# One filler unit moved from the end of one attention batch to the start of the next

## Chip, cores and metric

The kernel runs on one core of one Trainium2 chip. The metric is device time in microseconds (us). Before the change it was 326.37 us, the median of three runs (326.36 to 327.01).

A ratio in this document is the mean time of one kernel's fast runs over that of the other's fast runs of the same rounds, with a 95% interval. It is therefore not quite the ratio of the medians that are quoted beside it.

## The reference

Eight batches of sparse attention (8 heads, 576 tokens, head size 64, a window of 32 to each side, and 8 global tokens that see and are seen by all) are followed by a two-layer product with a squared relu over all 4608 tokens.

```python
scores = scale * np.matmul(q, k.transpose(0, 1, 3, 2))
mask = np.abs(pos[:, None] - pos[None, :]) <= window
mask = mask | is_global[:, None] | is_global[None, :]
...
attn_out = np.matmul(softmax(where(mask, scores, -1e9)), v)     # abridged
x = attn_out.transpose(0, 2, 1, 3).reshape(B * S, H * D)        # 4608 x 512
h = x @ w_in                                                     # 512 -> 2048
r = np.maximum(h, 0.0)
out = (r * r) @ w_out                                            # 2048 -> 512
```

## The kernel before

Attention works on pairs of heads, four pairs to a batch. It makes TensorE wait often: scores go to PSUM, ScalarE takes their exponential, VectorE masks them, and only then can TensorE multiply them with the values. The two-layer product is almost pure TensorE work. So its pieces, called **units**, stand in a queue and are taken as filler between the steps of a pair. A unit is four 128x512 matmuls: `mm1` makes 128 of the 2048 inner columns for a chunk of 512 tokens, `mm2` a quarter of one 128-row block of the result.

```python
def unit(i, n, nxt=None, then=None):                 # pair i; n = units taken at three places
    scs = [scores(i, half, pair_tag[half], WIN2) for half in range(2)]   # PSUM tiles sc, acc
    et = [weights(half, scs[half], WIN2) for half in range(2)]           # Exp, then mask
    ...
    take(n[0])
    ...
    for half in range(2):
        acc = outputs(i, half, et[half], pair_tag[half], WIN2, ...)      # sc, acc again
        finish_outputs(i, half, acc, ...)                                # to xT in SBUF
        if half == 0:
            take(n[1])
    if i % NHP == NHP - 1:
        scatter(i // NHP)                            # global tokens' columns into xT
    take(n[2])
```

A chunk has 512 tokens and a batch 576. Chunk 0 needs batch 0 alone, but chunk 1 needs the tokens of batch 1 as well: its first `mm1` can't run before batch 1's last outputs are in xT and the scatter is done. Whatever is left of a batch's queue is flushed at the batch's end.

```python
queue += units[1] + units[2]              # with one kept: 25 units of chunk 0
...
for hp in range(NHP):                     # batch 1
    unit(NHP + hp, SCHED["b1"][hp], ...)
...
for b in range(2, B):
    queue += units[b + 1]                 # 32 units of the next chunk
    for hp in range(NHP):
        n = ((2, 1, 4), (3, 1, 4), (2, 1, 5), (2, 1, 6)) if b < B - 1 else SCHED["last"]
        unit(NHP * b + hp, n[hp])
        ...
    take(99)
```

The end of an output half, as far as the argument needs it (VectorE executes in this order):

```python
# finish_outputs, second half of a batch's last pair (cut)
act.activation(out=rec[r], in_=av[xs][rs, :, 0:GTOK], func=AF.Ln)         # L702
act.activation(out=rec, in_=rec, func=AF.Exp, scale=-1.0)                 # L703
dve.tensor_reduce(out=gsum[b][...], in_=av[x][...], ...)                  # L720
dve.tensor_tensor(out=gs, in0=gsum[b][:, 0], in1=gsum[b][:, 1], ...)      # L726
global_outputs(b, gs, 0, NHP, columns)                                    # L690, L692
dve.tensor_tensor(out=xT[...], in0=av[x][...], in1=rec[r], op=ALU.mult)   # L732, last read of acc
# then scatter: eight small copies, L751; then the next pair's masks, L643
```

The softmax here doesn't subtract the row's maximum and nothing guards it: scores larger than these inputs give would overflow.

Of the kernel before, what the change touches and what calls it, by code (L numbers as in the profile page):

```python
# [39 lines left out]
)  # L40
W2 = 440
MB = (0, 456)
SCHED = dict(w8=2, w9=3, w5=3, w6=0, w7=4, wa=4, wb=3, wc=3, g0=1, w0=2, w1=4, w2=2, w3=2, w4=3, w=5, h0=0, h1=1, h4=1, h5=1, h2=1, h3=0, keep=1, b1=((3, 1, 3), (2, 1, 3), (2, 1, 3), (2, 1, 2)), last=((2, 1, 4), (3, 1, 4), (2, 1, 4), (2, 1, 7)))
ONES = 2.0**-7 * (1.0 + 15360.0 / 2**23)


# [1 line left out]
def kernel(  # L48
# [144 lines left out]
    def keep_warm(n):  # L193
        if n:
            w = pst("tr", [P, 512])
        for _ in range(n):
            nc.tensor.matmul(w, idle[:, 0:P], idle, start=True, stop=True)  # L197
# [8 lines left out]
    def indices():  # L206

        low = g64.bitcast(I32).rearrange("p (g two) -> p g two", two=2)[:, :, 0]
        clamped(g32c, 0, S - 1, low)
        nc.vector.tensor_copy(out=g16, in_=low)  # L210
        edges()
        gb = pst("mm", [P, 512])[:, 0:NG]
        nc.tensor.matmul(gb, ones, g16, start=True, stop=True)
        return gb
# [11 lines left out]
    def one_hots(gb):  # L226
        nc.vector.tensor_copy(out=gbf, in_=gb)
        nc.vector.tensor_tensor(
            out=oh, in0=gbf.unsqueeze(1).to_broadcast((P, NT, NG)),
            in1=tok.unsqueeze(2).to_broadcast((P, NT, NG)), op=ALU.is_equal,  # L230
        )
        nc.vector.tensor_tensor(
            out=ohp, in0=gbf.unsqueeze(1).to_broadcast((P, TJ, NG)),
            in1=tokp.unsqueeze(2).to_broadcast((P, TJ, NG)), op=ALU.is_equal,
        )
# [4 lines left out]
    def mask_natural(half):  # L240
        if 1:
            for t, so, c0, w in WIN[half]:
                for grp in range(4):
                    lo, hi = max(grp * GRP, c0), min(grp * GRP + GTOK, c0 + w)
                    o = MB[half] + so + lo - c0
                    if lo < hi:
                        u = lo - 8 * grp - KT * t + U0
                        nc.vector.tensor_copy(
                            out=mask[:, o : o + hi - lo], in_=ub[t // 4][:, u : u + hi - lo]
                        )  # L250
                    lo, hi = max(grp * GRP + GTOK, c0), min((grp + 1) * GRP, c0 + w)
                    o = MB[half] + so + lo - c0
                    if lo < hi:
                        nc.vector.tensor_copy(
                            out=mask[:, o : o + hi - lo],
                            in_=rows[:, t // 4 : t // 4 + 1].to_broadcast((P, hi - lo)),
                        )

    def mask_globals_matmul(half):
        mg = pst("acc" if half == 0 else "mm", [P, 1, 512])  # L260
        if 1:
            wins = [x for x in WIN[half] if x[3] > 8]
            for i, (t, so, c0, w) in enumerate(wins):
                o = c0 - half * BANKC
                nc.tensor.matmul(
                    mg[0:NG, 0, o : o + w], oh[:, t, :],
                    mask[:, MB[half] + so : MB[half] + so + w],
                    start=(i == 0), stop=(i == len(wins) - 1), skip_group_check=True,
                )
        return mg  # L270
# [161 lines left out]
    def cast_tokens(op, nm, hp):  # L432
        t = nat0[(nm, hp)] = sbt("nat0" + nm, [TP, TJ, P], FP16, bufs=2)
        op(out=t.rearrange("p j (h d) -> p h j d", h=2), in_=st[nm][0:TP, pair(hp)])
# [5 lines left out]
    def clear_value_rows():  # L440
        act.copy(
            out=vb[0][0:NG, :, 0 : 2 * H : 2],
            in_=idle[0:NG].rearrange("p (h d) -> p h d", d=D).unsqueeze(1).to_broadcast((NG, NT, H, D)),
        )
# [42 lines left out]
    def tr_k(i, op=None, tail=None, last=None, tag="mm", then=None):  # L487
        op = op or dve.tensor_copy
        tk, gl = transposed("k", i, tag)
        kt = kts[i % NHP]  # L490
        op(
            out=kt[:, 0:4, 8:P].rearrange("p t (q j) -> p t q j", j=TJ),
            in_=tk[:, 0:80].rearrange("p (t q) j -> p t q j", t=4),
        )
        if then:
            then()
        (tail or op)(
            out=kt[:, 4, 8 : 8 + KN[4]].rearrange("p (q j) -> p q j", j=TJ), in_=tk[:, 80:96]
        )
        (last or op)(out=kt[:, :, 0:NG], in_=gl.unsqueeze(1).to_broadcast((P, NT, NG)))  # L500

    def tr_q(i, op=None, tag="mm"):
        op = op or dve.tensor_copy
        tq, gl = transposed("q", i, tag)
        q4 = qts[i % NHP].rearrange("p (g x) -> p g x", x=GRP)
        op(
            out=q4[:, :, 0:GTOK].rearrange("p g (q j) -> p g q j", j=TJ),
            in_=tq.rearrange("p (g q) j -> p g q j", g=4),
        )
        op(out=q4[:, :, GTOK:GRP], in_=gl.unsqueeze(1).to_broadcast((P, 4, NG)))  # L510
# [252 lines left out]
    clear_value_rows()  # L763
    keep_warm(SCHED["w0"])
    gb = indices()
    fetch_globals()
    one_hots(gb)
    keep_warm(SCHED["w1"])
    mask_natural(0)
    mg = mask_globals_matmul(0)  # L770
    keep_warm(SCHED["w2"])
    cast_tokens(dve.tensor_copy, "k", 0)
# [5 lines left out]
    mg = mask_globals_matmul(1)  # L778
    keep_warm(SCHED["w3"])
    ets = {}  # L780

    def half0(i):
        tag = pair_tag[i % 2]
        ets[i] = exps(0, scores(i, 0, tag, WIN), WIN)
# [7 lines left out]
    cast_tokens(dve.tensor_copy, "q", 1)  # L792
    keep_warm(SCHED["w4"])
    tr_k(1, then=lambda: tr_q(1, act.copy))
    keep_warm(SCHED["w5"])
    tr_k(2, then=lambda: (half0(1), tr_q(2, act.copy)))
# [175 lines left out]
```

## Time and profile before

| | before |
|---|---|
| time, median | 326.37 us |
| TensorE busy | 316.8 us, 97% of the span |
| VectorE, ScalarE busy | 227.0 us (70%), 214.4 us (66%) |
| chain that ended last | 88% TensorE |
| a unit of four 128x512 matmuls | 0.86 us |
| stops of TensorE from the first second-product matmul (49.44 us) to the end | 0.20 us at 67.65 and 0.68 us at 69.50 |

A **stop** is here the distance of two matmuls' starts less what the first one takes when nothing is waited for (0.216 us for 512 columns); a change of matmul shape, which costs 0.10 us or less, is not counted. Stops are read from starts because a matmul's end in the profile is modelled. The list of waits counts from that end and so shows less, or nothing. The lines that matter are in the prediction.

### The profile page before, as it was taken

Reading aid. Unit: us, or ns where it says so; the run is one execution under the profiler, and the core shown is the slowest. Engines: PE = TensorE matmul, PEld = TensorE weight load, DVE = VectorE, ACT = ScalarE, POOL = GpSimd, SP = SyncE. Lnnn points to the kernel's source line nnn. Section 1 sums busy time; section 2 is a strip of 40 time slices with the busy share of each in tenths; the row PEclk is TensorE's granted clock in tenths of the full one; section 3 lists DMA queues with packets and bytes.
Section 4 is the critical chain, followed back from the end, with each engine's and each line's share of the span. In section 5 each row is a group of like instructions: output and inputs, shape, how many; then the busy total and the mean of one; then the engine's idle time right before and its main releaser. Section 6 shows DMA issues by size and latency. Waiting matters only on the chain.

```text
span 326.0 us, 6920 instructions
## 1 busy us (share of the span) xinstructions
PE 316.8 (97%) x2434; PEld 164.5 (50%) x2434; DVE 227.0 (70%) x674; ACT 214.4 (66%) x418; POOL 110.2 (34%) x148
## 2 busy tenths in 40 slices
PE   6998999999999999999999999999999999999996
PEld 2645775445555455455545544454455544444444
DVE  7786987677878875987598758885888675313421
ACT  6677985569954995499549954995499636404600
POOL 9824663639800870089107700680000000000000
PEclk9999999999999999999999999999999999999999
DMA  8999999999994999399959996999610011011012
GB/s 186 176 204 190 174 186 167 154 147 107 153 131 141 73 138 171 134 83 139 132 162 82 148 126 144 98 134 132 139 60 0 34 58 39 2 73 56 2 54 75
DMA packets 148229, 37.53 MB, mean 115 GB/s; under 512 B 136171, under 2 KB 143715, under 8 KB 148195
## 3 DMA queue, kind: packets, MB, share of 16 engines
q0 software_dynamic: 105168, 17.93, 78.9%
q1 hardware_dynamic: 42880, 19.04, 30.3%
q8 instruction: 19, 0.31, 0.4%
q10 hardware_dynamic: 146, 0.13, 0.1%
q14 instruction: 16, 0.12, 0.1%
HBM read 37.30 MB, written 17.05 MB: 167 GB/s over the span
## 4 chain that ended last, share of the span: by engine, by line
PE 88%; DVE 7%; ACT 2%; issue 1%; DMA 1%
PE mm L587 29%; PE mm L524 26%; PE tr L524 9%; PE tr L587 7%; PE sc L679 3%; PE acc L679 3%; PE sc L627 3%; PE mm L543 2%; PE acc L627 2%; DVE xT L751 2%; PE tr L197 1%; DVE vb L457 1%; PE sc L670 1%; DVE xT L732 1%; ACT rec L702 1%
## 5 line engine op out<-in xcount | busy, mean ns | idle before, releaser
L587 PE MATMUL mm<-w_out,gt 128*128 128x512 f16 x448 | 104.4, 379 | 0.0
L524 PE MATMUL mm<-xT,w_in 128*128 128x512 f16 x384 | 90.8, 379 | 0.5 <-DVE xT L751 0.5
L587 PEld LDWEIGHTS <-gt 128*128 128x128 f16 x560 | 52.4, 98 | 58.6
L524 PEld LDWEIGHTS <-w_in 128*128 128x128 f16 x512 | 47.5, 98 | 53.7 <-issue 0.8
L529 ACT ACTIVATE rl<-mm 128x512 f16<-128x512 f32 x96 | 54.3, 599 | 26.7 <-PE mm L524 26.7
L530 DVE TENSOR_TENSOR gt<-rl 128x512 f16<-128x512 f16 x128 | 51.0, 422 | 17.0 <-ACT rl L529 15.6
L636 ACT ACTIVATE et<-sc 128x880 f16<-128x880 f32 (+1 forms) x32 | 29.0, 907 | 44.1 <-PE sc L627 39.1
L643 DVE TENSOR_TENSOR et<-et,mask 128x880 f16<-128x880 f16 (+1 forms) x64 | 38.9, 615 | 24.1 <-ACT et L636 23.8
L113 POOL DMA_DIRECT2D vb<-in_v_dram x40 | 40.7, 1532 | 9.0 <-DMA w_in<-in_moe_w_in_dram 7.3
L524 PE MATMUL tr<-xT,w_in 128*128 128x512 f16 x128 | 33.0, 380 | 0.0
L564 DVE COPY ot<-mm 128x512 f32<-128x512 f32 (+1 forms) x29 | 19.7, 680 | 18.0 <-PE mm L587 16.3
L636 ACT ACTIVATE et<-acc 128x880 f16<-128x880 f32 (+1 forms) x32 | 29.1, 909 | 1.0 <-PE acc L627 1.0
L703 ACT ACTIVATE rec<-rec 128x288 f32<-128x288 f32 x64 | 28.3, 443 | 2.0
L732 DVE TENSOR_TENSOR xT<-sc,rec 64x288 f16<-64x288 f32 (+1 forms) x55 | 25.0, 455 | 6.5 <-ACT rec L703 6.2
L732 DVE TENSOR_TENSOR xT<-acc,rec 64x288 f16<-64x288 f32 (+1 forms) x55 | 25.0, 455 | 3.9 <-ACT rec L703 1.1
L404 POOL DMA_DIRECT2D scr_k<-in_k_dram x30 | 26.6, 1111 | 2.8 <-issue 2.8
L679 PEld LDWEIGHTS <-vb 128*128 128x128 f16 x288 | 21.3, 98 | 11.5
L930 POOL COPY pin<-gsh 1x1 f32<-1x1 f32 x5 | 0.9, 177 | 76.4 <-DVE gsh L720 76.4
L702 ACT ACTIVATE rec<-sc 64x288 f32<-64x288 f32 (+1 forms) x55 | 22.3, 406 | 6.2 <-PE sc L679 4.2
L404 POOL DMA_DIRECT2D scr_q<-in_q_dram x24 | 25.1, 1585 | 3.0 <-DMA w_out<-in_moe_w_out_dram 3.0
L587 PE MATMUL tr<-w_out,gt 128*128 128x512 f16 x112 | 25.3, 379 | 0.0
L702 ACT ACTIVATE rec<-acc 64x288 f32<-64x288 f32 (+1 forms) x55 | 22.2, 404 | 2.0 <-PE acc L670 1.1
(147 smaller groups left out, 308.5 us busy)
## 6 DMA issues: line engine op xcount, KB each, us to landing
out_dram<-ot SPq DMA_DIRECT2D x35, 256.0 KB
vb<-in_v_dram POOLq DMA_DIRECT2D x32, 120.0 KB, 11.3
scr_q<-in_q_dram POOLq DMA_DIRECT2D x24, 144.0 KB, 5.9
scr_k<-in_k_dram POOLq DMA_DIRECT2D x24, 120.0 KB, 4.2
w_in<-in_moe_w_in_dram POOLq DMA_DIRECT2D x4, 512.0 KB, 11.9
w_out<-in_moe_w_out_dram POOLq DMA_DIRECT2D x4, 512.0 KB, 12.3
natk<-in_k_dram POOLq DMA_DIRECT2D x3, 288.0 KB, 10.9
natq<-in_q_dram POOLq DMA_DIRECT2D x3, 288.0 KB, 15.8
```

Of the source, the lines that this page charges most:

```text
L113: pool.dma_start(out=vb[b][NG : NG + KN[x], x, 2 * hs.start : 2 * hs.stop : 2], in_=v[b, hs, x * KT : x * KT + KN[x]].rearrange("h s d -> ...
L404: pool.dma_start(out=scr[(nm, b % 2)][x * pitch + off : x * pitch + off + hi - lo].rearrange("s (h d) -> s h d", d=D), in_=src[nm][b, :, l ...
L524: nc.tensor.matmul(ph, w_in[:, t, u * P : (u + 1) * P], xT[:, t, XOFF + c * TC : XOFF + (c + 1) * TC], start=(t == 0), stop=(t == NDM - 1),)
L529: nc.scalar.activation(out=rl, in_=ph, func=AF.Relu)
L530: nc.vector.tensor_tensor(out=gts[c][:, u, :], in0=rl, in1=rl, op=ALU.mult)
L587: nc.tensor.matmul(po, gts[c][:, f, m * P : (m + 1) * P], w_out[:, f, :], start=(f == 0), stop=(f == NFF - 1),)
L636: act.activation(out=et[:, :, 0:W], in_=sc[:, :, 0:W], func=AF.Exp, bias=0.0, scale=scale)
L643: dve.tensor_tensor(out=et[:, :, 0:W], in0=et[:, :, 0:W], in1=mask[:, MB[half] : MB[half] + W].unsqueeze(1).to_broadcast((P, 2, W)), op=AL ...
L679: nc.tensor.matmul(banks[e][:, o : o + w], vtf[:, t, vo : vo + P], et[:, e, so : so + w], start=(n == 0), stop=(n == nw - 1), skip_group_c ...
L702: act.activation(out=rec[r], in_=av[xs][rs, :, 0:GTOK], func=AF.Ln)
L703: act.activation(out=rec, in_=rec, func=AF.Exp, scale=-1.0)
L732: dve.tensor_tensor(out=xT[r, hp, x0 : x0 + HS].rearrange("p (k x) -> p k x", k=2), in0=av[x][r, :, 0:GTOK], in1=rec[r], op=ALU.mult,)
```

## The change

Its intent is to leave one unit more of chunk 0 in the queue at the end of batch 1, so that batch 2's first pair has two units that wait for nothing in front of the first unit of chunk 1, which waits for the scatter.

```diff
-SCHED = dict(... b1=((3, 1, 3), (2, 1, 3), (2, 1, 3), (2, 1, 2)), ...)
+SCHED = dict(... b1=((3, 1, 3), (2, 1, 3), (2, 1, 3), (2, 1, 1)), ...)
```

More of the change, by code (lines that the diff above doesn't have):

```diff
@@ L42 @@
 MB = (0, 456)
-SCHED = dict(w8=2, w9=3, w5=3, w6=0, w7=4, wa=4, wb=3, wc=3, g0=1, w0=2, w1=4, w2=2, w3=2, w4=3, w=5, h0=0, h1=1, h4=1, h5=1, h2=1, h3=0, keep=1, b1=((3, 1, 3), (2, 1, 3), (2, 1, 3), (2, 1, 2)), last=((2, 1, 4), (3, 1, 4), (2, 1, 4), (2, 1, 7)))
+SCHED = dict(w8=2, w9=3, w5=3, w6=0, w7=4, wa=4, wb=3, wc=3, g0=1, w0=2, w1=4, w2=2, w3=2, w4=3, w=5, h0=0, h1=1, h4=1, h5=1, h2=1, h3=0, keep=1, b1=((3, 1, 3), (2, 1, 3), (2, 1, 3), (2, 1, 1)), last=((2, 1, 4), (3, 1, 4), (2, 1, 4), (2, 1, 7)))
 ONES = 2.0**-7 * (1.0 + 15360.0 / 2**23)
```

## The prediction

> **What bounds the kernel now.** I read the page's busy table first, then the chain of work that ended last, then the waits of TensorE, and last the timelines of TensorE and VectorE around the one place where the change acts, the end of batch 1.
>
> ```profile
> PE 316.8 (97%) x2434; PEld 164.5 (50%) x2434; DVE 227.0 (70%) x674; ACT 214.4 (66%) x418; POOL 110.2 (34%) x148
> ...
> PE 88%; DVE 7%; ACT 2%; issue 1%; DMA 1%
> ...
> PE mm L524 <- DVE xT L751: 0.5, 1, 0.5
> ```
>
> The first line is busy time by engine, the second the chain by engine, the third the only wait of TensorE that the profile finds between 55 and 110 us. TensorE is the bound: 97% busy, 88% of the chain. From 69.5 to 322 us the windows show it busy the whole time, so whatever is gained or lost before 69.5 us goes unreduced to the end. The change moves one piece of matmul work across the end of batch 1, so what matters is the time that TensorE stands still there. Its timeline (start, length, instruction; matmul ends are modelled, so I go by starts):
>
> ```profile
> 65.20 0.23 PE L670 MATMUL acc<-et,vb 128*64 128x136 f16 x2
> 65.26 0.23 PE L670 MATMUL acc<-et,one 128*64 128x136 f16 x2
> 65.42 1.90 PE L587 MATMUL mm<-w_out,gt 128*128 128x512 f16 x8
> 67.25 0.36 PE L627 MATMUL sc<-qb,kb 64*128 64x160 f16 x6
> 67.65 0.37 PE L627 MATMUL acc<-qb,kb 64*128 64x112 f16 x6
> 67.95 1.04 PE L587 MATMUL mm<-w_out,gt 128*128 128x512 f16 x4
> 69.50 1.02 PE L524 MATMUL mm<-xT,w_in 128*128 128x512 f16 x4 [0.51 <-DVE xT L751]
> 70.36 0.55 PE L679 MATMUL sc<-et,vb 128*128 128x160 f16 x6
> 70.74 1.03 PE L524 MATMUL mm<-xT,w_in 128*128 128x512 f16 x4
> 71.60 0.54 PE L679 MATMUL acc<-et,vb 128*128 128x112 f16 x6
> 71.98 1.03 PE L524 MATMUL mm<-xT,w_in 128*128 128x512 f16 x4
> ```
>
> VectorE over the same time:
>
> ```profile
> 65.08 0.45 DVE L732 TENSOR_TENSOR xT<-sc,rec 128x288 f16<-128x288 f32 x1
> 66.10 0.26 DVE L720 TENSOR_REDUCE gsh<-acc 128x8 f32<-128x16 f32 x2 [0.57 <-ACT rec L702]
> ...
> 67.14 0.45 DVE L732 TENSOR_TENSOR xT<-acc,rec 128x288 f16<-128x288 f32 x1
> 67.63 1.81 DVE L751 COPY xT<-gx 128x4 f16 x8
> 69.34 1.14 DVE L643 TENSOR_TENSOR et<-et,mask 128x880 f16<-128x880 f16 x2
> 70.40 0.68 DVE L564 COPY ot<-mm 128x512 f32<-128x512 f32 x1
> ```
>
> The reader is to see four events. The last attention outputs of batch 1 start at 65.26. Two units of chunk 0's second matrix product (x8) follow as filler. Then batch 2's first pair starts: its scores go to the two PSUM tiles called sc and acc, at 67.25 and 67.65. One more unit (x4) follows, and at 69.50 the first unit of chunk 1 starts, which reads the xT that batch 1 has just finished; it waits for the scatter (eight L751 copies, to 69.44).
>
> There are **two stops**, not one. A 128x512 matmul costs 0.216 us start to start (1.83 us for eight, less about 0.10 us at a change of matmul shape), so a unit of four is 0.86 us. The unit at 67.95 has given its last start's slot by 67.95 + 0.87 = 68.82, and the next starts at 69.50: a stop of 0.68 us. The wait view shows only 0.51, as it counts from the modelled end. The smaller stop is between the halves of the scores: six L627 matmuls take two by two about 0.20 us, so the acc half could start at 67.45, and it starts at 67.65: 0.20 us, not marked as a wait. It ends 0.06 us after VectorE's last read of acc (67.14 + 0.45 = 67.59).
>
> **What the Trainium skill says.** "PSUM — Partial Sum Buffer", section "Engine vs sequencer instructions": matmuls start and complete in program order. The timeline agrees: while the chunk 1 unit stands at its wait from 68.82 to 69.50, no later matmul passes it. The same page, "PSUM bank collisions raise a hardware error": guard PSUM by bank, because two engines must not be in one bank at once. This is why scores into acc wait for L732's read of acc; the 67.59 to 67.65 step agrees. "TensorE: Matmul & The Clock Gate", section "Wait — 56ns, not 53.3ns?" gives 215.7 ns start to start for 512 columns; here 216. Its section "What's actually happening" says that idling for a window of about 3.4 us lowers the clock; the granted clock stayed 1.00 through the present stop of 0.68 us, and none of the stops that I expect is near that length.
>
> **The change part by part.** The schedule has 24 units taken in batch 1's four pairs out of 25 queued; after the change 23, so that two units of chunk 0 are left, not one. Nothing is removed or added: the same matmuls, copies and transfers. It **moves** (a) one unit of 0.86 us from between batch 1's last outputs and batch 2's first scores, to after these scores; (b) every unit of batch 2 by one slot, so that the first chunk 1 unit comes after the first half of the outputs; (c) one unit more to the flush at the end of batch 2, after which all is as before.
>
> The intent is plain: the extra unit stands before the scatter-bound unit and fills its 0.68 us. Now the positions. VectorE's chain from outputs to scatter (65.26 on) depends on outputs that have not moved, so L732 on acc still ends at 67.59 and the scatter at 69.44.
> 1. The filler after the outputs is one unit: 65.42 + 0.86 + 0.10 = 66.38, and the sc scores start there (sc was read to 65.08 + 0.45 = 65.53, so it is free). They are through by 66.58.
> 2. The acc scores still can't start before 67.65. The stop there grows from 0.20 to 67.65 - 66.58 = 1.07 us. Loss 0.87. This is exactly the removed unit's 0.86: the filler stood in front of a wait that was nearly covered.
> 3. Two units now follow, from 67.95: eight matmuls, through at 67.95 + 0.01 + 1.73 = 69.69. The 0.68 us stop at the scatter is gone. Gain 0.68.
> 4. Next come the first outputs (L679 into sc), no longer the chunk 1 unit. They need the masked weights: the first L643 runs behind the scatter, 69.34 to about 69.95 (half of 1.14, plus the overlap). They start at about 70.00. New stop: 70.00 - 69.69 = 0.31. Loss 0.31.
> 5. The outputs take 0.38 (70.36 to 70.74 now): 70.38. The chunk 1 unit follows to 71.25, the second outputs to 71.63. Their mask is done by 70.48: no stop.
> Compare at the end of the second outputs: before 71.98 with two chunk 1 units done, after 71.63 with one. Lacking is one unit: 71.63 + 0.86 - 71.98 = **+0.51 us**. By stops: (1.07 + 0.31) - (0.20 + 0.68) = +0.50. The same.
>
> Is it taken up later? TensorE has no idle time after this, so no slack exists to absorb it. Does more come? The next pair's scores wait for acc to be read too: now at 75.28 against a need at 75.43. After the change the outputs are 0.35 us earlier, ScalarE has one relu (L529, 0.60) less in front of their Ln and Exp, and TensorE arrives at 71.63 + 4 x 0.86 = 75.1: covered by some 0.3 us. In the third pair of batch 2 three first-product units are left in place of two, the last between the two halves of the outputs. Its relu and square come behind two Ln (0.41 each), an Exp (0.44) and two L732 (0.46 each), ready some 3.3 us after those outputs; the second-product part that reads it comes after 0.86 + 0.38 + 3 x 0.86 = 3.8 us. It fits by about half a microsecond. Batches 3 and later begin with an empty queue and have a similar split (7 and 8 first-product units in the first two pairs) without stops.
>
> **The rivals.**
> (A) The intent works: 0.68 us saved, 325.7 us. For it: the wait view names only this wait. Against: the acc tile, which the view doesn't show because the removed unit hides it.
> (B) Nothing: stops only change places, 326.4 us. It would be so if L732 on acc finished earlier, or the masks ran before the scatter; program order on VectorE speaks against both.
> (C) Data for batch 2 come too late for the earlier scores and outputs. The landing events of the transposes that fill qb end at 63.13, needed at 66.38; the value fetches are issued from 60.07 to 63.69 and land about 4.7 us later, by 68.4, needed at 70.00. With 3.2 and 1.6 us to spare I give it little; it would make 327 to 328 us.
> (D) The shift by a slot makes ScalarE the bound in batch 2 (it is busy 4.95 of 5.00 us from 75 to 80 us). There is one relu less at first and one more later; if the half microsecond reckoned above for the third pair isn't there, up to 1 us more: 327.5 us.
>
> **Range and chances.** 326.37 + 0.5 = 326.9 us. The three runs of before spread over 0.65 us, the effect is no larger than that. The low end, 326.2, is B with a fast run; the high end, 327.7, is D or C in part. 2% is 6.5 us, more than ten times all stops concerned together, so within 2% is all but certain.
>
> **What would show it right or wrong.** Right: in TensorE's timeline the sc scores start near 66.4 and the acc scores still at 67.65, a marked wait of about 0.9 to 1.1 us behind L732; eight L587 matmuls from 67.95; no wait for L751; the first L679 at about 70.0 behind L643; the span longer by about 0.5 us. Wrong: acc scores clearly before 67.6, or an L679 start before 69.9 (then B or A), or new stops after 72 us (then D), or a DMA named as releaser (then C).

## The result, and the profile after

The changed kernel took 326.77 us (median of four runs, 326.70 to 327.05) against 326.60 us (326.36 to 327.01) for the kernel before in the same rounds: a ratio of 1.0006, interval 0.9988 to 1.0023. It is the same within 2%, and 326.77 lies in the range, close to the 326.9 that was predicted. The interval is too wide to tell half a microsecond from nothing; two later timings of the same kernel, below, gave 1.0023 and 1.0031.

The span of the profiled run fell, from 326.0 to 325.3 us, though the time did not. This is the start: before, TensorE waited 1.1 us for a VectorE instruction (L213) about three microseconds in, and after, it didn't. The change can't reach that far back. So I compare from the first second-product matmul on: before, it starts at 49.44 in a span of 326.05, which leaves 276.61 us; after, at 48.13 in a span of 325.28, which leaves 277.15 us. That is **0.54 us more**.

The page of the kernel after, busy time and chain by engine:

```profile
PE 316.3 (97%) x2434; PEld 164.2 (50%) x2434; DVE 227.0 (70%) x674; ACT 214.5 (66%) x418; POOL 110.2 (34%) x148
...
PE 89%; DVE 7%; ACT 2%; issue 1%
```

The same counts of instructions, the same bound. The waits of TensorE in the kernel after (waiting instruction, what released it, us in total, times, longest), those two that concern the end of batch 1:

```profile
PE acc L627 <- DVE xT L732: 0.8, 1, 0.8
...
PE sc L679 <- DVE et L643: 0.3, 1, 0.3
```

The wait for the scatter (L524 for L751) is gone from the list. Two others stand in its place: the scores into acc wait for VectorE's last read of acc, and the first outputs wait for the mask. TensorE's timeline of the kernel after (start, length, instruction):

```profile
63.95 0.23 PE L670 MATMUL acc<-et,one 128*64 128x136 f16 x2
64.11 1.04 PE L587 MATMUL mm<-w_out,gt 128*128 128x512 f16 x4
65.08 0.36 PE L627 MATMUL sc<-qb,kb 64*128 64x160 f16 x6
66.21 0.37 PE L627 MATMUL acc<-qb,kb 64*128 64x112 f16 x6 [0.77 <-DVE xT L732]
66.51 1.90 PE L587 MATMUL mm<-w_out,gt 128*128 128x512 f16 x8
68.67 0.62 PE L679 MATMUL sc<-et,vb 128*128 128x160 f16 x6 [0.26 <-DVE et L643]
69.12 1.03 PE L524 MATMUL mm<-xT,w_in 128*128 128x512 f16 x4
```

VectorE in the same run: the last read of acc, the scatter, and the masks behind it:

```profile
65.71 0.45 DVE L732 TENSOR_TENSOR xT<-acc,rec 128x288 f16<-128x288 f32 x1
66.19 1.91 DVE L751 COPY xT<-gx 128x4 f16 x8
68.00 1.14 DVE L643 TENSOR_TENSOR et<-et,mask 128x880 f16<-128x880 f16 x2
```

The order is the predicted one. From 65.08 to 66.21 are 1.13 us where six score matmuls take 0.20: a stop of 0.93 us. From 66.51, eight matmuls take 1.73 us, and the outputs start at 68.67: a stop of 0.42 us. Together 1.36 us, against 0.20 + 0.68 = 0.87 us before (0.196 and 0.673 by the unrounded starts): 0.48 us more. From here to the end there is no stop over 0.15 us in either trace.

Now the chain that ended last, in order of time (start, length, what). Before, around the first unit of chunk 1:

```profile
69.26 0.19 DVE xT L751
69.45 0.04 issue
69.50 1.02 PE mm L524 x4
```

After, around the first outputs of batch 2:

```profile
67.93 0.18 DVE xT L751
68.10 0.52 DVE et L643
68.62 0.04 issue
68.67 0.62 PE sc L679 x6
```

In both, the chain runs along VectorE, from batch 1's last outputs through reductions, reciprocal and scatter. Before, it leaves VectorE after the scatter. After, it passes one mask more, 0.52 us, and only then returns to TensorE. The scores that waited 0.93 us for acc are **not on the chain** at all. That made me doubt how the prediction had put its step 2, where the acc tile is what costs.

### The profile page after: what moved, and what is told of

Read it like the earlier page. It is cut to its first block, busy times and chain, and to the rows that moved or that the text cites. A ratio compares the mean times of both kernels' runs of the same rounds, so it can differ in the third digit from the quotient of the medians.

```text
span 325.3 us, 6920 instructions
## 1 busy us (share of the span) xinstructions
PE 316.3 (97%) x2434; PEld 164.2 (50%) x2434; DVE 227.0 (70%) x674; ACT 214.5 (66%) x418; POOL 110.2 (34%) x148
## 4 chain that ended last, share of the span: by engine, by line
PE 89%; DVE 7%; ACT 2%; issue 1%
PE mm L587 29%; PE mm L524 26%; PE tr L524 9%; PE tr L587 7%; PE sc L679 3%; PE acc L679 3%; PE sc L627 3%; PE mm L543 2%; PE acc L627 2%; DVE xT L751 2%; PE tr L197 1%; PE sc L670 1%; DVE xT L732 1%; ACT rec L702 1%; PE acc L670 1%
## 5 line engine op out<-in xcount | busy, mean ns | idle before, releaser
L587 PE MATMUL mm<-w_out,gt 128*128 128x512 f16 x448 | 104.2, 379 | 0.0
L524 PE MATMUL mm<-xT,w_in 128*128 128x512 f16 x384 | 90.5, 379 | 0.0
L587 PEld LDWEIGHTS <-gt 128*128 128x128 f16 x560 | 52.5, 98 | 58.8
L524 PEld LDWEIGHTS <-w_in 128*128 128x128 f16 x512 | 47.4, 98 | 52.9
L524 PE MATMUL tr<-xT,w_in 128*128 128x512 f16 x128 | 32.9, 380 | 0.0
L732 DVE TENSOR_TENSOR xT<-sc,rec 64x288 f16<-64x288 f32 (+1 forms) x55 | 25.0, 455 | 6.5 <-ACT rec L703 6.2
L732 DVE TENSOR_TENSOR xT<-acc,rec 64x288 f16<-64x288 f32 (+1 forms) x55 | 25.0, 455 | 3.9 <-ACT rec L703 1.1
L587 PE MATMUL tr<-w_out,gt 128*128 128x512 f16 x112 | 25.3, 379 | 0.0
```

Of the source, the lines that this page charges most:

```text
L524: nc.tensor.matmul(ph, w_in[:, t, u * P : (u + 1) * P], xT[:, t, XOFF + c * TC : XOFF + (c + 1) * TC], start=(t == 0), stop=(t == NDM - 1),)
L587: nc.tensor.matmul(po, gts[c][:, f, m * P : (m + 1) * P], w_out[:, f, :], start=(f == 0), stop=(f == NFF - 1),)
L732: dve.tensor_tensor(out=xT[r, hp, x0 : x0 + HS].rearrange("p (k x) -> p k x", k=2), in0=av[x][r, :, 0:GTOK], in1=rec[r], op=ALU.mult,)
```

## The experiments

Three theories:

- **T1**, the prediction's steps taken word for word: the loss comes from the acc tile, whose last read the moved unit used to cover.
- **T2**: at the end of a batch TensorE has only so much work that waits for nothing. It runs out of it whatever its order, and the total of the stops is set by when the first dependent piece in its order is ready. Acc is only where part of the stop shows.
- **T3**: these stops don't reach the end of the kernel.

The results together; "acc" is the stop before the scores into acc, the other stops are named by what was waited for:

| run | median us | before, same rounds | ratio (95%) | stops at the end of batch 1 and after, us |
|---|---|---|---|---|
| the change, first | 326.77 | 326.60 | 1.0006 (0.9988 to 1.0023) | acc 0.93, mask 0.42 |
| r1_change | 327.64 | 327.23 | 1.0023 (1.0005 to 1.0040) | acc 1.60, mask 0.19 |
| c_change_again | 327.51 | 326.70 | 1.0031 (1.0015 to 1.0047) | acc 1.13, mask 0.23 |
| r2_two_left | 329.78 | 327.23 | 1.0062 (1.0040 to 1.0083) | 0.17 at the sc scores, acc 2.67, then half clock |
| r3_unit_first | 327.58 | 327.23 | 1.0017 (1.0003 to 1.0032) | acc 1.11, mask 0.46, next pair's acc 0.27 |
| r3b_unit_first | 327.19 | 327.22 | 1.0003 (0.9982 to 1.0023) | acc 0.93, mask 0.27, next pair's acc 0.27 |
| r4_early_read | 327.84 | 327.23 | 1.0027 (1.0008 to 1.0047) | acc 0.37, mask 0.96 |
| r5_early_and_first | 327.58 | 327.22 | 1.0002 (0.9980 to 1.0023) | acc 1.11, scatter 0.17, next pair's acc 0.52 |
| b_before_again | 327.21 | 327.22 | 1.0001 (0.9978 to 1.0024) | scatter 0.58, mask 0.54 |
| r6_kept_from_pair3 | 326.72 | 327.22 | 0.9974 (0.9953 to 0.9995) | mask 0.93 |
| r6b_kept_from_pair3 | 325.87 | 326.70 | 0.9983 (0.9965 to 1.0000) | none over 0.15 |
| r7_one_more | 327.19 | 326.70 | 1.0016 (1.0000 to 1.0033) | scatter 0.66; 0.12 and 0.34 at the start of batch 3 |
| r9_kept_and_first | 326.15 | 326.70 | 0.9981 (0.9967 to 0.9995) | 0.26 before the third pair's outputs |

All were correct. They ran each on one chip: r1 to r4; then b, r3b, r5 and r6; then c, r7, r6b and r9.

### The change, timed again (r1_change, c_change_again)

No edit: the changed kernel as it is.

> The change as it is, timed closely. Theory T1 (the prediction's steps: the acc tile's read is the cause) and theory T2 (TensorE has too little work that waits for nothing; the total of the stops is set by when the first dependent piece in its order becomes ready, and the acc tile is only where it shows) both expect 0.5 us more than before, a ratio of about 1.0015. Theory T3 (the stops don't reach the end, the time is the same) expects 1.000.

> The change once more, for a third timing beside its rivals on one chip: T1 and T2 expect 0.5 us more than before (1.0015), in the range 1.0005 to 1.003 that the earlier timings gave; T3 1.000. In the trace, the stop at acc at 0.9 to 1.6 us, depending on whether ScalarE's Ln and Exp start late again.

Both intervals lie above 1.000, and with the first they give 0.2, 0.75 and 1.0 us more (ratios times 326.6 us). T3 is out, and so is the rival "nothing". The third timing lies above the range of 1.0005 to 1.003 by a hair. The trace of c_change_again repeats the first one: stops of 1.13 and 0.23 us, 1.35 together, and from the first second-product matmul (48.00) to the end of the span (325.16) 277.16 us, again 0.55 more than before. The two also differ in a telling way: the acc stop is 0.20 us longer here and the mask stop 0.20 shorter, and in both the first outputs of batch 2 start 4.72 us after batch 1's last outputs (68.67 less 63.95 there, 68.54 less 63.82 here). The trace of r1_change does not repeat the first: its stops sum to 1.79 us, since ScalarE's Ln of the last outputs began 0.71 us after their end in it, against 0.04, and everything behind it on VectorE moved back. (Its Exp of the sc scores began late too, but ended at 67.93, before the mask's start at 68.37.) More on this below.

### The change doubled (r2_two_left)

```diff
-b1=((3, 1, 3), (2, 1, 3), (2, 1, 3), (2, 1, 1))
+b1=((3, 1, 3), (2, 1, 3), (2, 1, 3), (2, 1, 0))
```

> The change doubled: two units fewer after batch 1's last outputs, none left there. The acc scores' stop should grow from 0.93 to about 1.8 us, the stop at the mask stay at about 0.4: T1 and T2 expect 1.3 to 1.4 us more than before (ratio about 1.0042), far enough from noise to be seen. T3: 1.000.

The ratio is 1.0062, so 2.0 us more: the direction was right, the size over half as large again. The acc stop was 2.67 us, not 1.8, again with a late Ln (it starts 0.98 us after the outputs' end). And something came that neither theory had. The windows of this run (us, then busy time and number of instructions of TensorE, its weight loads, VectorE, ScalarE and GpSimd, then the granted TensorE clock, DMA share and GB/s):

```profile
67.00:68.00 1.00, 0.95 (x9) 0.42 (x9) 0.83 (x5) 0.07 (x1) 0.00 (x0) 0.79 0.95 225
68.00:69.00 1.00, 1.00 (x4) 0.43 (x3) 0.72 (x5) 1.00 (x2) 0.00 (x0) 0.50 0.22 25
```

After the stop the clock fell to half, for 3.4 us in all (0.79 is the mean of a microsecond in which it fell; 0.50 stands to 71.00). Seen by starts, the eight L587 matmuls stand 0.43 us apart, not 0.216. Seven such steps of 0.21 us too much make 1.5 us of the loss in this trace: this stop cost more than its length.

The timed runs tell the same. Four of the six have a mean clock of 0.993 to 0.995, as half clock for 3.4 us of 326 gives, and took 329.63 to 330.35 us; the other two have 0.998, too high for that, and took 328.07 and 328.47, about 1.0 us more than before. So most of the excess over the expected 1.3 to 1.4 us comes with the clock; the stops alone, on these two runs, cost no more than was expected.

### The chunk 1 unit in front again (r3_unit_first, r3b_unit_first)

```diff
+            if b == 2 and hp == 0:
+                n = ((3, 1, 3),)
```

This is on top of the change; seven units in this pair as before.

> The change, and the first chunk 1 unit goes in front of batch 2's first outputs again (three units there, three at the pair's end; as many in all). The stop at the mask (0.42 us) should go, as the chunk 1 unit needs only the scatter and stands in its place; the acc scores' stop stays at 0.93. T1 and T2: 0.1 us more than before (stops 0.93 and a few hundredths, against 0.87), so 0.4 less than the change. If the mask's stop is no real term, the time stays at the change's 0.5 more.

> The same kernel as r3_unit_first, again. There the mask's stop stayed (0.46), but because the Exp of the sc scores began 2.7 us after they were done. Without such a late update T1 and T2 expect an acc stop of 0.93 to 1.1, no stop behind it over 0.1, and a time within 0.2 us of before; with it again, an L679 wait for the mask of about 0.4 and 0.5 to 0.9 us more than before.

The two timings give 1.0017 and 1.0003, that is 0.55 and 0.1 us; the second is what was expected, the first is not, and their intervals overlap. Both traces still show a mask stop, because in both the Exp of the sc scores began late, 2.7 and 2.3 us after the scores. Both also show a new stop of 0.27 us at the next pair's scores, which the prediction had reckoned as covered "by some 0.3 us" in the change, and which this edit uncovers. So these two runs don't settle how much the mask's place is worth.

### Acc read earlier (r4_early_read), and both edits (r5_early_and_first)

This is the run that tells T1 from T2. VectorE's last read of acc goes in front of the reciprocal and the product of the global sums. The instruction and its data are the same and stay in front of the scatter.

```diff
                 dve.tensor_tensor(out=gs, in0=gsum[b][:, 0], in1=gsum[b][:, 1], op=ALU.add)
+                if b == 1:
+                    to_xT(b, hp, half, parts, av, rec)     # the L732 loop, as a function
                 global_outputs(b, gs, 0, NHP, columns)
+                if b == 1:
+                    return
+        to_xT(b, hp, half, parts, av, rec)
```

> The change, with VectorE's last read of the acc tile (the xT multiply) moved ahead of the reciprocal and the product of the global sums, so that acc is free about 0.5 us earlier relative to the outputs; the scatter ends about where it did (0.1 later at most). This tells T1 from T2. T1: the acc stop falls from 0.93 to about 0.45 and the gain stays, so about the time of before (ratio 1.000). T2: the acc stop falls as far, but TensorE then runs into the mask earlier, whose stop grows from 0.42 to about 0.9: the total of the stops stays at 1.35 or so, 0.5 us more than before (1.0015).

TensorE's timeline of r4_early_read:

```profile
64.94 0.36 PE L627 MATMUL sc<-qb,kb 64*128 64x160 f16 x6
65.51 0.37 PE L627 MATMUL acc<-qb,kb 64*128 64x112 f16 x6 [0.20 <-DVE xT L739]
65.81 1.90 PE L587 MATMUL mm<-w_out,gt 128*128 128x512 f16 x8
68.51 0.62 PE L679 MATMUL sc<-et,vb 128*128 128x160 f16 x6 [0.80 <-DVE et L643]
```

The acc stop fell from 0.93 to 0.37 us, as both theories said. But the stop at the mask grew from 0.42 to 0.96. Together they are 1.33 us, as in the change (1.36), and the timing is 1.0027, with 1.000 outside the interval. **T1 falls, T2 holds**: freeing acc sooner only lets TensorE reach the next wait sooner. (The Exp was late here too, by 1.6 us: it ends at 67.80, and the mask starts at 67.84. But it costs the mask little, since the scatter in front of it on VectorE ends at 67.76, and in the two traces of the change without a late Exp the mask started 0.1 us before the scatter's end. At most 0.2 of the 0.96 us are the Exp's.)

> The change with both edits: acc read earlier and the chunk 1 unit first. T2: the acc stop is about 0.4, then the chunk 1 unit waits for the scatter about 0.4; the total is what before has, 0.85 to 0.95, the time within 0.1 us of before. T1, by which the acc wait alone costs, would have 0.4 to 0.5 us less than before.

The timing, 1.0002, is T2's; T1's 0.4 to 0.5 us gain (0.9985) lies in the interval as well, so it alone proves nothing. Its trace doesn't show the expected stops, as the Ln of the last outputs began 0.79 us late.

### One unit more at the end of batch 1 (r7_one_more)

```diff
-b1=((3, 1, 3), (2, 1, 3), (2, 1, 3), (2, 1, 1))
+b1=((3, 1, 3), (2, 1, 3), (2, 1, 3), (2, 1, 3))
```

> The opposite of the change: one unit more after batch 1's last outputs (three), none left for batch 2. T1, counting the acc wait alone, would have a gain of up to 0.2 us as that wait goes. T2: the free work is as much as in before, so the acc stop (0.20) goes and the scatter's stop grows from 0.68 to about 0.9: the same total, a ratio of 1.000.

The acc stop is gone and the scatter's is 0.66 us (0.75 with the usual shape change). T2 had said 0.9, reckoned from the first trace of the kernel before; here the scatter ended 3.94 us after the last outputs' start, there 4.18, and that is the difference. Yet the time is 1.0016, half a microsecond more than before. The trace says where, for the greater part. TensorE's timeline at the start of batch 3:

```profile
101.44 1.89 PE L524 MATMUL mm<-xT,w_in 128*128 128x512 f16 x8
103.51 0.62 PE L679 MATMUL sc<-et,vb 128*128 128x160 f16 x6 [0.18 <-DVE et L643]
```

Here 101.44 holds a stop of 0.12 us (0.21 with the usual shape change) and 103.51 one of 0.34. The unit that batch 1 used up is missing in the flush at the end of batch 2, where it stood behind the scatter of batch 2. I had not followed the queue that far. With the one unit that the kernel before hands on there is no stop at that boundary, and this explains the other side too: the change hands on two, and the second one has no stop left to fill there.

### The unit taken from elsewhere (r6_kept_from_pair3, r6b_kept_from_pair3, r9_kept_and_first)

If T2 is right, only more free work at the boundary helps. Between 46 and 67 us, in batch 1, TensorE has no stops at all before the last pair is through, so it may have units to give there.

```diff
-b1=((3, 1, 3), (2, 1, 3), (2, 1, 3), (2, 1, 2))     # before
+b1=((3, 1, 3), (2, 1, 3), (2, 1, 2), (2, 1, 3))
```

> Before, but the unit is held back from batch 1's third pair instead, to stand after the last outputs: three units there, one left for batch 2. By T2 this adds 0.86 us of free work in front of the scatter's wait: stops of about 0.1 in place of 0.87, at the price of perhaps 0.1 us at the fourth pair's scores: 0.7 us less than before (ratio 0.998). If the third pair had no room to give (its masks or banks not ready), an equal stop appears between 54 and 62 us and the time is that of before. T3 (stops don't reach the end): 1.000 with the stops gone.

> The version that was faster, again: ratio 0.997 to 0.998 if the gain is real, no acc and no scatter stop; the stop at the mask 0 to 0.9 us, as the Exp of the sc scores is late or not.

Both timings gain: 0.9974 and 0.9983, 0.85 and 0.55 us less than before. TensorE's timeline of r6b_kept_from_pair3:

```profile
65.90 0.36 PE L627 MATMUL sc<-qb,kb 64*128 64x160 f16 x6
66.10 0.35 PE L627 MATMUL acc<-qb,kb 64*128 64x112 f16 x6
66.39 1.04 PE L587 MATMUL mm<-w_out,gt 128*128 128x512 f16 x4
67.38 1.02 PE L524 MATMUL mm<-xT,w_in 128*128 128x512 f16 x4
```

Each step starts when the one before is through; the only traces left of a wait are 0.11 us at 67.38 and, as expected, 0.12 us at the fourth pair's scores (59.10). The stops went from 0.87 to 0.23 us, 0.64 less, and from the first second-product matmul (47.95) to the end (323.95) it is 276.0 us, 0.6 less than before. (The trace of r6 does not show the gain: it has a late Exp, and a mask stop of 0.93 us.) This version beats both kernels, by under 0.3%; the second interval just touches 1.0000.

The fourth experiment of that call adds a chunk 1 unit in front of the first outputs of batch 2:

```diff
+            if b == 2:
+                n = ((3, 1, 4), (2, 1, 4), (2, 1, 5), (2, 1, 6))
```

> The faster version, with batch 2's first pair taking three, one and four units and its second two, one and four, so that one more chunk 1 unit stands before the first outputs, where the late Exp's stop of 0.93 us was. If late updates cost time in timed executions too, this gains up to 0.8 us more (ratio 0.995); if they don't, the time is that of the faster version (0.9975), or up to 0.3 us longer where the second pair's scores have to wait for acc.

It gives 0.9981, the same as r6b (0.9983). None of the four traces of this call had the late Exp that the edit is meant to cover, so there was nothing for it to gain. Whether it helps where the Exp is late stays open.

### The kernel before, traced again (b_before_again)

No edit.

> The kernel before itself, for its trace on the chip of this call and as a measure of noise: ratio 1.000. In the last call the change, whose program was the same as in its first trace, had TensorE's semaphore update for the sc scores reach ScalarE 1.3 us late, and 0.7 us late for the last outputs. If that is a matter of the chip or the execution (T4), this run may show late updates between 63 and 69 us too, with its two stops larger than 0.20 and 0.68; if it belongs to the change's order, the two stops are as they were and no Ln or Exp of ScalarE starts over 0.3 us after its scores or outputs there.

The ratio is 1.0001. But its trace is not that of the first call. TensorE's timeline and ScalarE's, of this run:

```profile
66.24 0.36 PE L627 MATMUL sc<-qb,kb 64*128 64x160 f16 x6
...
68.05 0.90 ACT L636 ACTIVATE et<-sc 128x880 f16<-128x880 f32 x1 [2.65 <-PE mm L587]
```

The scores into sc are done at 66.60, and the Exp that reads them starts at 68.05, 1.4 us late; behind it the mask is late, and the outputs stop for 0.54 us. So the late start is not the change's doing. It is a matter of the chip or the execution: I find it, by 0.6 to 2.7 us (counted from the end of the sc scores, or of ScalarE's work before the Exp where that is later), in all eight traces of the first two calls, and in none of the four of the third call or the two of the first results.

## Why the prediction was right

**The time** was right: 326.9 us predicted, 326.77 measured, and of the later timings two show the loss clear of zero. The half microsecond stands in both traces of the change without a late Exp, 0.54 and 0.55 us, against the one trace of the kernel before without one.

**Step 1**, the sc scores 1.12 us after the last outputs' start (66.38 less 65.26): 1.13 measured (65.08 less 63.95).

**Step 2**, the acc stop: 1.07 predicted, 0.93 measured. VectorE's last read of acc ended 2.21 us after those outputs' start (65.71 + 0.45 less 63.95) in place of 2.33, as the Ln began 0.13 us sooner. The prediction puts this wait down to a rule on PSUM banks; the scores also overwrite the columns of acc that VectorE is reading, so they would have to wait in any case.

**Step 3** was as predicted: no scatter stop.

**Step 4**, the mask stop: 0.31 predicted, 0.42 measured; the scatter took 1.91 us instead of 1.81, while TensorE came there sooner.

**Step 5**, the sum, +0.50 by stops: 0.48 measured. The errors of steps 2 and 4 have opposite signs, and T2 says why that must be: what TensorE doesn't lose at acc it loses at the mask.

**What was put wrongly** is the reading of step 2: "Loss 0.87. This is exactly the removed unit's 0.86: the filler stood in front of a wait that was nearly covered." The amounts add up, but the acc tile isn't the cause. r4_early_read took 0.56 us off that stop, and no time was gained. It also answers rival B, which was to come true "if L732 on acc finished earlier". Both orders have the same three units and the same scores to fill the gap with. Before, the first dependent piece is the chunk 1 unit, which needs the scatter; after the change it is the first outputs, which need the mask behind it on VectorE. The difference is that mask, 0.52 us on the chain. The prediction had this mask as a small extra loss in step 4; by the chains of the two traces it is the whole net loss. This last point is read from the traces: the runs meant to take the mask out of the order (r3, r3b, r5) were disturbed by late starts of ScalarE and do not prove it.

**The rivals.** A (the intent works) is out: the scatter stop did go, and nothing was gained by it. B (nothing) is out by r1_change and c_change_again. C (data too late) is not seen: no transfer is named in TensorE's waits there. D (ScalarE the bound in batch 2) is not seen in the change, whose traces have no stop after 70 us; the slack at the second pair, put at 0.3 us, was larger in the first trace of the change, where VectorE's read of acc ended at 73.37 and the scores into it started at 74.12. In r3_unit_first, whose outputs come later, it is used up and there is a stop of 0.27 us.

## What to carry to other kernels

Where several waits follow one another along one engine, filling one of them moves the stop to the next: count the work that waits for nothing and ask when the first dependent piece in the order becomes ready, rather than how long the longest listed wait is. A filler is only worth moving if it comes from a place where the bound engine has room to give, and it must be followed through the queue to the next boundary. Freeing a buffer sooner gains nothing while the consumer of the next result is the one that is late.

## What the Trainium skill lacked or had wrong

- "TensorE: Matmul & The Clock Gate", section "What's actually happening": the clock is said to fall after at least one idle window of about 3.4 us. In r2_two_left a stop of 2.67 us was enough: the granted clock was 0.79 in the following microsecond and 0.50 in the next three, with matmuls 0.43 us apart. It fell at about 67.6, and the 3.4 us before that hold the stop, six scores before it and the matmuls from 67.05 on, so they were not idle throughout. Four of six timed runs show the lower clock (0.993 to 0.995) and two do not (0.998).
- "Perfetto Trace Analysis", section "Tensor Engine Instruction (MATMUL, LD_WEIGHTS)": it says that the semaphore update is pushed and spread after the modelled end, but gives no size for this. Here ScalarE's Ln of the last outputs followed their modelled end by 0.04 us (after) and 0.17 us (before), yet in eight traces the Exp of one pair's scores came 0.6 to 2.7 us late; in r1_change the trace's record of TensorE's update stands at 67.00, just before the Exp at 67.03, though the scores were through at 65.37. No run here shows the cause. The DMA engines were as busy there in traces without it (share 2.35 from 65 to 66 us in the change's first trace) as in those with it (2.26 in r1_change).
